# A recurrence and two feed-forward stages: from block 3 on every product in halves of 64 rows, two side by side

## The chip, the core and the metric

The kernel runs on one core of one Trainium2 chip. The metric is the device time of one execution in microseconds (us). TensorE does the matrix products, VectorE (DVE), ScalarE (ACT) and GpSimd (POOL) the elementwise work, SyncE (SP) mostly issues transfers. Weight loads of TensorE stand in the profile as an engine of their own, PEld.

## The reference: what is computed

A gated recurrence over 768 steps for 2 x 8 heads of width 40 gives an activation of 1536 tokens x 320. Two feed-forward stages follow, and they are what the change is about:

```python
# first stage: 4 experts, F = 1024, weighted by p
for e in range(E):
    h = np.maximum(x @ w1[e], 0.0)
    out += p[:, e:e + 1] * (h @ w2[e])
# second stage: d_ff = 1536
a = x @ w_a
b = x @ w_b
return (a * b @ w_out)
```

All in float32. The kernel takes each operand of a product as a high and a low part (`wh`, `wl` of the weights, `xh`, `xl` of the activation, `hh`, `hl` of the hidden values) and sums three of the four partial products.

## The kernel before, in words

**Blocks.** The hidden units are cut into 14 blocks. Blocks 0 to 7 belong to the first stage (two blocks of 4 x 128 hidden units for each expert), blocks 8 to 13 to the second (2 x 128 units each, with an `a` and a `b` product for each). Blocks 0 to 2 run interleaved with the recurrence, 256 tokens at a time (`Item`), and stay as they are. From block 3 on nothing else is left for TensorE; the tokens come in three groups `c` of 512. A **unit**, as the text calls it, is one block with one token group: 11 blocks x 3 groups = 33 units, 15 of the first stage and 18 of the second.

**First product of a unit (class `Pair`, method `a`).** Four sums, each in a PSUM bank of 128 x 512: four slices `f` of hidden units in the first stage, `b0, a0, b1, a1` in the second. The inner dimension is 320 = 128 + 128 + 64. A sum takes seven matmuls with all 128 rows (`mm_most`, line 214; the third row slice holds the 64 remaining weight rows twice, and `xh` there has the high part above the low part), and one more product, the low weights of the last 64 rows. For this last one two sums share a step: `mm_rest` (lines 219 and 220) issues a 64-row matmul in the upper half and another in the lower half of the array, for two different sums. `xq` is a copy of the 64 high rows on the lower partitions (`shift_x`). The sums 2 and 3 of a unit get theirs at its end, and together with them the sums 0 and 1 of the next unit get theirs as a first term (`begun`). Five units are named in `APART` and do without: there the last product is an eighth matmul of 128 rows (`mm_group`, line 207), and so it is where no `begun` sum was made.

**Eviction.** ReLU on ACT and the low part on DVE (lines 306, 307), or `bs`, `g`, `hh`, `hl` by turns on ACT and DVE in the second stage (lines 310 to 314).

**Second product (method `b`, lines 261 to 263).** For each of the four token tiles `t` of a unit three matmuls of 128 rows x 320 columns for each slice of hidden units: 48 in a unit of the first stage, 24 in one of the second. `Stream` runs it two items behind the first product. DVE then adds the sum to `acc` (lines 321, 783).

**Weights.** `piece1` and `piece2` are generators that load a piece of a block by a DMA on SP's queue (lines 86 and 104) and split it into `wh` and `wl` on ACT, DVE and POOL in the steps after. `Paced.step` advances them; `PACE` says after how many steps the next piece opens (1.5 for the first 32 pieces, which are blocks 4 to 7; 2.4 and 2.5 after). There are 8 steps in a unit of the first stage and 4 in one of the second. The raw pieces of the first stage go round two buffers, those of the second three. The order on each engine is the order in which the program writes its instructions.

**Between the stages** the 12 token tiles of `acc` are transposed back (`finish_x2`) and split. PSUM has eight banks: `Turns` takes four for the first product (`"a"`) and four for the second (`"b"`).

Of the kernel before, what the change touches and what calls it, by code (L numbers as in the profile page):

```python
# [18 lines left out]
P = 128  # L19
# [21 lines left out]
APART = ((NB1 - 1, 1), (NB1 - 1, 2), (NB1, 0), (NB1, 1), (NB1 + NB2 - 1, 2))  # L41
# [6 lines left out]
def mlstm_moe_kernel(ctx, tc, gates, qk, qc, kvo, dp, w1b, w2b, ident_d, bdmask_d, rsel_d, exp_d, out):  # L48
# [24 lines left out]
    def piece1(i, s, pool, lo_eng, apart=False):  # L73


        if s == 0:
            wblk[i] = (pool.tile([P, WB1], F32R, tag="wh", name=f"wh{i}"), pool.tile([P, WB1], F32R, tag="wl", name=f"wl{i}"))
        wh, wl = wblk[i]
        st = WB1 // NP1
        cs = slice(s * st, (s + 1) * st)  # L80
        if i < 3:
            at = (s if i == 0 else 8 + s if s < 2 else s) * st
            raw = sums[:, at:at + st]
        else:
            raw = rawp.tile([P, st], F32, tag="raw", name=f"raw{i}_{s}")
        nc.sync.dma_start(raw, w1b[i][:, cs])
        yield
        if apart:
            yield
        nc.scalar.copy(wh[:, cs], raw)  # L90
        yield
        lo_eng.tensor_tensor(wl[:, cs], raw, wh[:, cs].bitcast(F32), op=ALU.subtract)  # L92

    def piece2(i, s, pool):
# [9 lines left out]
        nc.sync.dma_start(raw.rearrange("p n w -> p (n w)"), w2b[i - NB1].bitcast(I32)[:, 2 * s * st:2 * (s + 1) * st])  # L104
# [21 lines left out]
    def split_x(ps, c, o):  # L126

        split_hi(ps, c, o)
        split_lo(ps, c, o)
# [9 lines left out]
    def shift_x(c):  # L139

        nc.gpsimd.dma_start(xq[c][64:128, :], xh[c][0:64, 2, :])
# [67 lines left out]
    def mm_most(ps, wh, wl, o0, c, start):  # L209

        k = lambda w, t: w[:, o0 + t * P:o0 + (t + 1) * P]
        prs = [(wh, 0, xh, 0), (wh, 1, xh, 1), (wh, 2, xh, 2), (wl, 0, xh, 0), (wl, 1, xh, 1), (wh, 0, xl, 0), (wh, 1, xl, 1)]
        for i, (w, t, x, u) in enumerate(prs):
            nc.tensor.matmul(ps, k(w, t), x[c][:, u, :], start=start and i == 0, stop=not start and i == len(prs) - 1)  # L214

    def mm_rest(psa, psb, wl, oa, ob, c, start):

        oa, ob = oa + 2 * P, ob + 2 * P
        nc.tensor.matmul(psa, wl[0:64, oa:oa + P], xh[c][0:64, 2, :], start=start, stop=not start)  # L219
        nc.tensor.matmul(psb, wl[64:128, ob:ob + P], xq[c][64:128, :], start=start, stop=not start)  # L220

    class Item:
# [5 lines left out]
        def a(self):  # L228
            blk, f, c, o, n = self.blk, self.f, self.c, self.o, self.n
            pa, ph = self.pools["a"], self.pools["h"]  # L230
            wh, wl = wblk[blk]
            self.hh = ph.tile([P, n], F32R, tag="hh", name="hh")
            self.hl = ph.tile([P, n], F32R, tag="hl", name="hl")
            if blk < NB1:
                ps = pa.tile([P, 512], F32, tag="a", name="psa")[:, :n]
                mm_group(ps, wh, wl, f * WF1, c, o, n)
                nc.scalar.activation(self.hh, ps, AF.Relu)  # L237
                nc.vector.scalar_tensor_tensor(self.hl, ps, 0.0, self.hh.bitcast(F32), op0=ALU.max, op1=ALU.subtract)  # L238
            else:
                pb = pa.tile([P, 512], F32, tag="a", name="psb")[:, :n]  # L240
                mm_group(pb, wh, wl, f * WF2 + 384, c, o, n)
                bs = ph.tile([P, n], F32, tag="bs", name="bs", bufs=2)
                nc.scalar.copy(bs, pb)
                ps = pa.tile([P, 512], F32, tag="a", name="psa")[:, :n]
                mm_group(ps, wh, wl, f * WF2, c, o, n)
                g = ph.tile([P, n], F32, tag="g", name="g", bufs=2)
                nc.vector.tensor_tensor(g, ps, bs, op=ALU.mult)
                nc.scalar.copy(self.hh, g)
                nc.vector.tensor_tensor(self.hl, g, self.hh.bitcast(F32), op=ALU.subtract)

        def b(self):
            blk, f, fi, nf, n = self.blk, self.f, self.fi, self.nf, self.n
            wh, wl = wblk[blk]
            off = f * WF1 + 384 if blk < NB1 else f * WF2 + 768
            if fi == 0:
                last = (blk, self.c) == (NB1 + NB2 - 1, 2)
                self.pools["bt"] = [self.pools[q].tile([P, DM], F32, tag=q, name="psy") for q in ("aabb" if last else "bbbb")[:n // P]]
# [8 lines left out]

    begun = {}

    class Pair(Item):

        def a(self):
            blk, f, c, one = self.blk, self.f, self.c, self.blk < NB1
            wh, wl = wblk[blk]
            pa, ph = self.pools["a"], self.pools["h"]
            new = lambda b, g: pa.tile([P, 512], F32, tag="a", name="psa" if b < NB1 or g % 2 else "psb")
            at = lambda b, g: g * WF1 if b < NB1 else g // 2 * WF2 + (g % 2 == 0) * 384
            self.q, ready = {}, [self]  # L280
            for g in [f] if one else [2 * f, 2 * f + 1]:
                if (blk, c, g) in begun:
                    self.q[g] = begun.pop((blk, c, g))
                    mm_most(self.q[g], wh, wl, at(blk, g), c, False)
                    continue
                self.q[g] = new(blk, g)
                if g < 2 or (blk, c) in APART:
                    mm_group(self.q[g], wh, wl, at(blk, g), c, 0, 512)
                    continue
                mm_most(self.q[g], wh, wl, at(blk, g), c, True)  # L290
                if g == 2:
                    ready = []
                    continue
                ready = [self.prev, self] if one else [self]
                p2 = self.prev.q[2] if one else self.q[2]
                mm_rest(p2, self.q[3], wl, at(blk, 2), at(blk, 3), c, False)
                nb, nc_ = (blk, c + 1) if c < 2 else (blk + 1, 0)
                for h in range(2):
                    begun[nb, nc_, h] = new(nb, h)
                mm_rest(begun[nb, nc_, 0], begun[nb, nc_, 1], wblk[nb][1], at(nb, 0), at(nb, 1), nc_, True)  # L300
            for it in ready:
                it.hh = ph.tile([P, 512], F32R, tag="hh", name="hh")
                it.hl = ph.tile([P, 512], F32R, tag="hl", name="hl")
                if one:
                    ps = it.q[it.f]
                    nc.scalar.activation(it.hh, ps, AF.Relu)  # L306
                    nc.vector.scalar_tensor_tensor(it.hl, ps, 0.0, it.hh.bitcast(F32), op0=ALU.max, op1=ALU.subtract)  # L307
                else:
                    bs = ph.tile([P, 512], F32, tag="bs", name="bs", bufs=2)
                    nc.scalar.copy(bs, it.q[2 * f])  # L310
                    g = ph.tile([P, 512], F32, tag="g", name="g", bufs=2)
                    nc.vector.tensor_tensor(g, it.q[2 * f + 1], bs, op=ALU.mult)  # L312
                    nc.scalar.copy(it.hh, g)
                    nc.vector.tensor_tensor(it.hl, g, it.hh.bitcast(F32), op=ALU.subtract)
# [447 lines left out]
    pools = {"a": Turns(ps_a2, ps_a), "b": Turns(ps_b2, ps_b), "h": hp2}  # L762
    todo, twice = [], {}

    def finish_x2(n):
        pt = pools["a"].tile([P, 512], F32, tag="a", name="pt_x2")
        pv = pt[:, 0:384].rearrange("p (k t) -> p k t", t=P)
        transpose_x(acc[n], twice[n], pv)
        split_x(pv, n // 4, (n % 4) * P)
        if n % 4 == 3:  # L770
            shift_x(n // 4)

    def done2(blk, n, ps):
        if blk < NB1:
            add_expert(blk, n, ps)
            if blk == NB1 - 1:
                twice[n] = hp2.tile([P, P], F32, tag="twice", name="twice", bufs=4)
                nc.scalar.copy(twice[n].rearrange("p (a b) -> p a b", a=2), acc[n][:, 256:].unsqueeze(1).to_broadcast([P, 2, 64]))
                todo.append(n)
# [13 lines left out]
    prev = None  # L793
    for blk in range(3, NB1 + NB2):
        nf = 4 if blk < NB1 else 2
        for c in range(3):
            for f in range(nf):
                ready = list(todo)

                def finish(k):  # L800
                    for n in ready[:k]:
                        ready.remove(n)
                        todo.remove(n)
                        finish_x2(n)

                def between():
                    paced.step()
                    if blk == NB1:
                        finish(2)

                item = Pair(blk, f, f, nf, c, 0, 512, pools, done2)
                item.prev, prev = prev, item
                stream.push(item, between)
                paced.step()
                finish(2)
    stream.flush()
# [102 lines left out]
```

## Time and profile before

| | us |
|---|---|
| median of 3 runs | 635.52 (635.46 to 637.06) |
| span of the profiled execution (its own time isn't listed beside the three) | 633.8 |
| TensorE busy | 621.0 (98%) |
| VectorE busy | 419.4 (66%) |
| ScalarE busy | 266.7 (42%) |
| GpSimd busy | 186.0 (29%) |

The profile is of one execution. Busy time of TensorE counts a matmul from its start to its modelled end, and matmuls overlap; how fast it really goes is read from the distance between the starts of two matmuls. The chain that ended last names, at each moment, the work that the end of the span hung on.

### The profile page before, as it was taken

How to read it: one execution, taken by the hardware profiler on the slowest of the kernel's cores; microseconds unless marked ns; L12 is line 12 of the kernel's file. 1: busy time of each engine (PE TensorE's matmuls, PEld its weight loads, DVE VectorE, ACT ScalarE, POOL GpSimd, SP SyncE). 2: the span in 40 equal slices, each digit the busy share in tenths (PEclk: the TensorE clock that was granted, in tenths of full speed). 3: DMA queues.
4: the chain of work that ended last, by engine and by line, in shares of the span. 5: the costliest groups of instructions: out<-in, count | busy, mean ns of one | idle time of the engine just before them, and what ended most of it. 6: DMA issues, size and time to landing. Idle time of an engine off the chain costs nothing.

```text
span 633.8 us, 10305 instructions
## 1 busy us (share of the span) xinstructions
PE 621.0 (98%) x3799; PEld 553.1 (87%) x3799; DVE 419.4 (66%) x860; ACT 266.7 (42%) x592; POOL 186.0 (29%) x223
## 2 busy tenths in 40 slices
PE   9898999999999999999999999999999999999997
PEld 6788999999999888888888888888888888888886
DVE  8889959596753244332788887888656776854344
ACT  6665464646333233332433344544543433422121
POOL 4686342424111011233233333333222222220000
PEclk9998999999999999999999999999999999999999
DMA  7882443435203122323221222221111111000003
GB/s 218 240 231 74 116 118 95 120 99 125 55 12 78 35 69 58 79 59 109 57 71 54 71 57 68 70 64 44 45 54 35 55 36 35 19 1 1 1 3 123
DMA packets 27967, 46.77 MB, mean 74 GB/s; under 512 B 3285, under 2 KB 17869, under 8 KB 27917
## 3 DMA queue, kind: packets, MB, share of 16 engines
q1 hardware_dynamic: 27437, 45.33, 26.2%
q0 software_dynamic: 480, 0.79, 0.6%
q8 instruction: 30, 0.49, 0.3%
q14 instruction: 20, 0.16, 0.1%
HBM read 43.35 MB, written 1.97 MB: 72 GB/s over the span
## 4 chain that ended last, share of the span: by engine, by line
PE 90%; DVE 6%; ACT 2%; issue 1%; POOL 1%; ACTq 0%; DVEq 0%; POOLq 0%
PE psa L214 20%; PE psa L207 14%; PE psy L261 13%; PE psy L263 11%; PE psy L262 11%; PE psb L214 8%; PE pt_y L503 3%; PE pt_c L485 2%; PE psb L207 2%; PE psb L219 1%; PE psa L219 1%; PE pt_i L509 1%; PE pt_a L475 1%; PE pt_w L590 1%; PE pt_u L553 1%
## 5 line engine op out<-in xcount | busy, mean ns | idle before, releaser
L261 PE MATMUL psy<-wh,hh 128*128 128x320 f32 x528 | 169.1, 320 | 0.6 <-DVE acc L321 0.6
L263 PE MATMUL psy<-wh,hl 128*128 128x320 f32 x528 | 163.2, 309 | 0.0
L262 PE MATMUL psy<-wl,hh 128*128 128x320 f32 x528 | 163.1, 309 | 0.0
L261 PEld LDWEIGHTS psy<-wh,hh 128*128 128x128 f32 x528 | 99.6, 189 | 15.5 <-issue 12.1
L262 PEld LDWEIGHTS psy<-wl,hh 128*128 128x128 f32 x528 | 99.7, 189 | 2.6
L263 PEld LDWEIGHTS psy<-wh,hl 128*128 128x128 f32 x528 | 99.4, 188 | 0.0
L307 DVE SCALAR_TENSOR_TENSOR hl<-psa,hh 128x512 fp32r<-128x512 f32 x60 | 40.2, 689 | 74.4 <-ACT hh L306 73.9
L124 POOL TENSOR_TENSOR wl<-tp,lf 128x272 fp32r<-128x272 f32 x48 | 38.8, 808 | 122.2 <-DVE tp L123 122.2
L214 PE MATMUL psa<-xh,wh 128*128 128x512 f32 x246 | 70.1, 393 | 0.0
L207 PE MATMUL psa<-xh,wh 128*128 128x256 f32 (+1 forms) x258 | 65.8, 309 | 0.4 <-ACT xh L132 0.4
L306 ACT ACTIVATE hh<-psa 128x512 fp32r<-128x512 f32 x60 | 34.5, 597 | 72.4 <-PE psa L214 41.3
L207 PE MATMUL psa<-xh,wl 128*128 128x256 f32 (+1 forms) x258 | 63.9, 302 | 0.0
L237 ACT ACTIVATE hh<-psa 128x256 fp32r<-128x256 f32 x72 | 27.6, 383 | 75.0 <-PE psa L207 73.5
L312 DVE TENSOR_TENSOR g<-psa,bs 128x512 f32<-128x512 f32 x36 | 24.8, 688 | 49.3 <-ACT bs L310 35.0
L121 POOL TENSOR_TENSOR lf<-lf,sq 128x272 f32<-128x272 f32 x48 | 37.2, 776 | 67.8 <-ACT wh L120 34.0
L92 POOL TENSOR_TENSOR wl<-raw,wh 128x352 fp32r<-128x352 f32 x28 | 26.6, 956 | 96.4 <-ACT wh L90 83.9
L214 PE MATMUL psa<-xh,wl 128*128 128x512 f32 x164 | 51.2, 393 | 0.0
L214 PE MATMUL psa<-xl,wh 128*128 128x512 f32 x164 | 50.8, 391 | 0.0
L238 DVE SCALAR_TENSOR_TENSOR hl<-psa,hh 128x256 fp32r<-128x256 f32 x72 | 30.3, 420 | 30.7 <-ACT hh L237 30.4
L214 PEld LDWEIGHTS psa<-xh,wh 128*128 128x128 f32 x246 | 44.0, 188 | 6.0
L310 ACT COPY bs<-psb 128x512 f32<-128x512 f32 x36 | 21.1, 587 | 62.7 <-PE psa L220 35.0
L207 PEld LDWEIGHTS psa<-xh,wh 128*128 128x128 f32 x258 | 45.2, 191 | 2.1 <-ACT xh L132 0.7
(139 smaller groups left out, 1168.0 us busy)
## 6 DMA issues: line engine op xcount, KB each, us to landing
raw<-in_w2b SPq DMA_DIRECT2D x48, 272.0 KB, 2.8
qk_t<-in_qk SPq DMA_DIRECT2D x16, 480.0 KB, 6.9
raw<-in_w1b SPq DMA_DIRECT2D x40, 176.0 KB, 2.3
acc<-in_w1b SPq DMA_DIRECT2D x24, 176.0 KB, 3.5
kvo_t<-in_kvo SPq DMA_DIRECT2D x10, 364.5 KB, 4.8
og_t<-in_kvo SPq DMA_DIRECT2D x6, 320.0 KB, 5.7
out<-acc SPq DMA_DIRECT2D x12, 160.0 KB, 1.8
qc_t<-in_qc SPq DMA_DIRECT2D x10, 180.0 KB, 3.6
```

The lines of the kernel that those rows point to most:

```text
L92: lo_eng.tensor_tensor(wl[:, cs], raw, wh[:, cs].bitcast(F32), op=ALU.subtract)
L121: nc.gpsimd.tensor_tensor(lf, lf, sq, op=ALU.mult)
L124: nc.gpsimd.tensor_tensor(wl[:, cs], tf, lf, op=ALU.add)
L207: nc.tensor.matmul(ps, l, r, start=(i == 0), stop=(i == len(prs) - 1))
L214: nc.tensor.matmul(ps, k(w, t), x[c][:, u, :], start=start and i == 0, stop=not start and i == len(prs) - 1)
L237: nc.scalar.activation(self.hh, ps, AF.Relu)
L238: nc.vector.scalar_tensor_tensor(self.hl, ps, 0.0, self.hh.bitcast(F32), op0=ALU.max, op1=ALU.subtract)
L261: nc.tensor.matmul(ps, lh, wh[:, off:off + DM], start=(fi == 0), stop=False)
L262: nc.tensor.matmul(ps, lh, wl[:, off:off + DM], start=False, stop=False)
L263: nc.tensor.matmul(ps, ll, wh[:, off:off + DM], start=False, stop=(fi == nf - 1))
L306: nc.scalar.activation(it.hh, ps, AF.Relu)
L307: nc.vector.scalar_tensor_tensor(it.hl, ps, 0.0, it.hh.bitcast(F32), op0=ALU.max, op1=ALU.subtract)
```

## The change

From block 3 on `Pair`, `mm_most`, `mm_rest`, `begun` and `APART` go. A unit's first product is `quad_a`: all its matmuls have 64 rows, and two always stand side by side, one on the upper 64 partitions (`UP`) and one on the lower (`DN`), for two different sums in two banks. In four phases the pairs of sums are (0,1), (2,3), (1,0), (3,2) as upper and lower; a phase has 8, 8, 7 and 7 pairs. The second product is `quad_b`, in the same way over token tiles. Since two halves may not be in one bank at once, the third and fourth phase must come behind the first and second: `leave` puts an empty instruction on SP that waits for the last matmul of a phase, and `behind` makes the first matmul of the phase two later wait for it. The second product of a unit runs behind the first product of the next unit; the evictions of slices 0 and 1 stand ahead of it, those of 2 and 3 in its middle. `hh` and `hl` have six buffers each. The DMAs of weight pieces from block 4 on are issued on ACT's queue. The transposes between the stages are done for four tiles at once, in banks of the second product. The last unit's second product is done with 128 rows.

```diff
-    def piece1(i, s, pool, lo_eng, apart=False):
+    def piece1(i, s, pool, lo_eng, apart=False, dma=None):
...
-        nc.sync.dma_start(raw, w1b[i][:, cs])
+        (dma or nc.sync).dma_start(raw, w1b[i][:, cs])
...
-        nc.sync.dma_start(raw.rearrange("p n w -> p (n w)"), w2b[i - NB1].bitcast(I32)[:, 2 * s * st:2 * (s + 1) * st])
+        nc.scalar.dma_start(raw.rearrange("p n w -> p (n w)"), w2b[i - NB1].bitcast(I32)[:, 2 * s * st:2 * (s + 1) * st])
...
+    def behind(later, earlier):
+        tc.add_manual_dep(later.ins, earlier.ins.name, mybir.DependencyInfo(mybir.DependencyClass.Sync, mybir.DependencyReason.DATA), reason="row groups take turns in a bank")
+
+    def leave(m):
+        word = nc.sync.nop()
+        behind(word, m)
+        return word
+
+    def quad_a(blk, c, ps, hook):
+
+        wh, wl = wblk[blk]
+        at = [g * WF1 if blk < NB1 else g // 2 * WF2 + (g % 2 == 0) * 384 for g in range(4)]
+        terms = [(wh, 0, xh), (wh, 1, xh), (wl, 0, xh), (wl, 1, xh), (wh, 0, xl), (wh, 1, xl), (wh, 2, xh), (wl, 2, None)]
+
+        def half(g, i, rows, start, stop):
+            w, t, x = terms[i]
+            x = x[c][rows, t, :] if x else xh[c][rows, 2, :] if rows.start == 0 else xq[c][rows, :]
+            o = at[g] + t * P
+            return nc.tensor.matmul(ps[g], w[rows, o:o + P], x, start=start, stop=stop)
+
+        left = {}
+        for k, (up, dn) in enumerate(((0, 1), (2, 3), (1, 0), (3, 2))):
+            n = 8 if k < 2 else 7
+            for i in range(n):
+                top = half(up, i, UP, k < 2 and i == 0, k >= 2 and i == n - 1)
+                low = half(dn, i, DN, k < 2 and i == 0, k >= 2 and i == n - 1)
+                if i == 0 and k >= 2:
+                    behind(top, left[k - 2])
+                if i == n - 1 and k < 2:
+                    left[k] = leave(low)
+                hook(8 * k + i)
+
+    def quad_b(blk, fs, nf, h, ps, hook):
+
+        wh, wl = wblk[blk]
+        pairs = ((0, 1), (2, 3), (1, 0), (3, 2)) if fs[0] % 4 == 0 else ((1, 0), (3, 2), (0, 1), (2, 3))
+        left = {}
+        for k, two in enumerate(pairs):
+            for f in fs:
+                off = f * WF1 + 384 if blk < NB1 else f * WF2 + 768
+                hh, hl = h[f]
+                for i, (l, w) in enumerate(((hh, wh), (hh, wl), (hl, wh))):
+                    start, stop = k < 2 and f == 0 and i == 0, k >= 2 and f == nf - 1 and i == 2
+                    ms = [nc.tensor.matmul(ps[t], l[rows, t * P:(t + 1) * P], w[rows, off:off + DM], start=start, stop=stop) for t, rows in zip(two, (UP, DN))]
+                    if k >= 2 and f == fs[0] and i == 0:
+                        behind(ms[0], left[k - 2])
+            if k < 2:
+                left[k] = leave(ms[1])
+            else:
+                hook()
 
...
-    pools = {"a": Turns(ps_a2, ps_a), "b": Turns(ps_b2, ps_b), "h": hp2}
...
+    pa, pb = Turns(ps_a2, ps_a), Turns(ps_b2, ps_b)
+    twice = {}
+
+    def finish_x2(c):
+        for n in range(4 * c, 4 * c + 4):
+            pt = pb.tile([P, 512], F32, tag="b", name="pt_x2")
+            pv = pt[:, 0:384].rearrange("p (k t) -> p k t", t=P)
+            transpose_x(acc[n], twice[n], pv)
+            split_x(pv, c, (n % 4) * P)
+        shift_x(c)
...
-    pieces = [piece1(i, s, slot[i], nc.vector if LOENG.get(i, ())[s:s + 1] == "v" else nc.gpsimd, True) for i in range(4, NB1) for s in range(NP1)]
+    pieces = [piece1(i, s, slot[i], nc.vector if LOENG.get(i, ())[s:s + 1] == "v" else nc.gpsimd, True, nc.scalar) for i in range(4, NB1) for s in range(NP1)]
...
+    def evict(blk, ps, f):
+        if blk >= NB1:
+            bs, g = (hp2.tile([P, 512], F32R, tag=t, name=n, bufs=HB).bitcast(F32) for t, n in (("hh", "bs"), ("hl", "g")))
+        hh, hl = (hp2.tile([P, 512], F32R, tag=t, name=t, bufs=HB) for t in ("hh", "hl"))
+        if blk < NB1:
+            nc.scalar.activation(hh, ps[f], AF.Relu)
+            nc.vector.scalar_tensor_tensor(hl, ps[f], 0.0, hh.bitcast(F32), op0=ALU.max, op1=ALU.subtract)
+        else:
+            nc.scalar.copy(bs, ps[2 * f])
+            nc.vector.tensor_tensor(g, ps[2 * f + 1], bs, op=ALU.mult)
+            nc.scalar.copy(hh, g)
+            nc.vector.tensor_tensor(hl, g, hh.bitcast(F32), op=ALU.subtract)
+        return hh, hl
...
+    units = [(blk, c) for blk in range(3, NB1 + NB2) for c in range(3)]
...
+    for u, (blk, c) in enumerate(units):
+        at = (14, 29) if blk >= NB1 else (7, 14, 22, 29)
+        ready = u - 2 - 3 * (NB1 - 4)
+
+        def hook(j):
+            if j in at:
+                paced.step()
+            if j == 15 and 0 <= ready < 3:
+                finish_x2(ready)
+
+        ps = [pa.tile([P, 512], F32, tag="a", name="psa" if blk < NB1 or g % 2 else "psb") for g in range(4)]
+        quad_a(blk, c, ps, hook)
+        h = [evict(blk, ps, f) for f in range(2)]
         nf = 4 if blk < NB1 else 2
...
+        if last:
+            b0, c0, h0 = last
+            n0 = len(h0)
+            py = [pb.tile([P, DM], F32, tag="b", name="psy") for _ in range(4)]
+            quad_b(b0, (0, 1), n0, h0, py, paced.step)
+        else:
+            stream.flush()
+        h += [evict(blk, ps, f) for f in range(2, nf)]
+        if last:
+            if n0 > 2:
+                quad_b(b0, (2, 3), n0, h0, py, paced.step)
+            for t in range(4):
+                done2(b0, 4 * c0 + t, py[t])
+        last = (blk, c, h)
+    blk, c, h = last
+    wh, wl = wblk[blk]
+    for t in range(4):
+        ps = pa.tile([P, 512], F32, tag="a", name="psy")[:, 0:DM]
+        for f in range(2):
+            hh, hl = (x[:, t * P:(t + 1) * P] for x in h[f])
+            off = f * WF2 + 768
+            nc.tensor.matmul(ps, hh, wh[:, off:off + DM], start=f == 0, stop=False)
+            nc.tensor.matmul(ps, hh, wl[:, off:off + DM], start=False, stop=False)
+            nc.tensor.matmul(ps, hl, wh[:, off:off + DM], start=False, stop=f == 1)
+        done2(blk, 4 * c + t, ps)
```

## Rows read from the trace of the kernel before

**Rows 1.** The page, engines: busy us, share of the span, instructions.

```profile
PE 621.0 (98%) x3799; PEld 553.1 (87%) x3799; DVE 419.4 (66%) x860; ACT 266.7 (42%) x592; POOL 186.0 (29%) x223
```

**Rows 2.** The page, chain that ended last: shares of the span by engine.

```profile
PE 90%; DVE 6%; ACT 2%; issue 1%; POOL 1%; ACTq 0%; DVEq 0%; POOLq 0%
```

**Rows 3.** Chain that ended last, 296 to 340 us: start us, us, what.

```profile
306.06 1.61 PE psa L214 x7
307.67 0.42 PE psa L219
308.10 0.23 PE psa L219
308.33 0.35 PE psy L261
...
318.26 0.47 DVE acc L321
...
318.87 0.38 PE psy L261
```

**Rows 4.** Timeline of PE, 300 to 309 us: start us, us, instruction, count.

```profile
300.78 0.30 PE L261 MATMUL psy<-wh,hh 128*128 128x320 f32 x1
...
302.53 0.39 PE L214 MATMUL psa<-xh,wh 128*128 128x512 f32 x1
...
305.90 0.86 PE L214 MATMUL psa<-xh,wh 128*128 128x512 f32 x3
...
307.60 0.49 PE L219 MATMUL psa<-xh,wl 64*128 64x512 f32 x1
...
307.94 0.39 PE L219 MATMUL psa<-xh,wl 64*128 64x512 f32 x1
...
308.52 0.30 PE L262 MATMUL psy<-wl,hh 128*128 128x320 f32 x1
```

**Rows 5.** Instructions of line 219: idle time of their engine before them, times.

```profile
  issue: 10.0, 28
```

**Rows 6.** Timeline of PEld (weight loads), 305.8 to 309.2 us.

```profile
307.60 0.18 PEld L219 LDWEIGHTS psa<-xh,wl 64*128 64x128 f32 x1 [0.35 <-issue]
307.60 0.18 PEld L220 LDWEIGHTS psa<-xq,wl 64*128 64x128 f32 x1
307.71 0.19 PEld L219 LDWEIGHTS psa<-xh,wl 64*128 64x128 f32 x1
307.71 0.19 PEld L220 LDWEIGHTS psa<-xq,wl 64*128 64x128 f32 x1
```

**Rows 7.** Timeline of PE, 104.3 to 107 us: short matmuls, each with its load.

```profile
104.42 1.91 PE L503 MATMUL pt_y<-kvo_t,w_t 128*128 128x82 f32 x16
106.17 0.87 PE L509 MATMUL pt_i<-cbd_t,qc_t 120*128 120x123 f32 x6
106.79 0.39 PE L261 MATMUL psy<-wh,hh 128*128 128x320 f32 x1
```

**Rows 8.** Windows: us, PE, PEld, DVE, ACT, POOL busy (x), PEclk, DMA share, GB/s.

```profile
100.00:120.00 20.00, 20.00 (x163) 19.91 (x163) 15.01 (x33) 10.12 (x21) 10.79 (x11) 1.00 0.50 126
...
340.00:360.00 20.00, 20.00 (x114) 17.71 (x113) 17.02 (x33) 8.73 (x21) 7.69 (x10) 1.00 0.26 70
360.00:380.00 20.00, 19.61 (x108) 16.67 (x107) 17.81 (x38) 7.02 (x18) 6.86 (x9) 1.00 0.22 57
```

**Rows 9.** Timeline of ACT, 307 to 309 us: idle before, and its releaser.

```profile
308.19 1.09 ACT L306 ACTIVATE hh<-psa 128x512 fp32r<-128x512 f32 x2 [1.88 <-PE psa L220]
```

**Rows 10.** Waits of SP's queue: waiter, releaser, us in total, times, longest.

```profile
SPq L104 <- DVE tp L115: 226.6, 45, 11.3
...
SPq L86 <- POOL wl L92: 61.7, 31, 9.3
```

**Rows 11.** Instructions of line 104: duration ns min/median/max, first and last start.

```profile
L104 SPq DMA_DIRECT2D raw<-in_w2b x48: 327/328/432, 296.7 to 542.3; - x48
```

**Rows 12.** The page, DMA issues: count, KB each, median us to landing.

```profile
raw<-in_w2b SPq DMA_DIRECT2D x48, 272.0 KB, 2.8
```

More of the change, by code (lines that the diff above doesn't have):

```diff
@@ L40 @@
 PACE = ((0, 1.5), (32, 2.4), (62, 2.5))
-APART = ((NB1 - 1, 1), (NB1 - 1, 2), (NB1, 0), (NB1, 1), (NB1 + NB2 - 1, 2))
+UP, DN = slice(0, 64), slice(64, 128)
+HB = 6
 NEG = -1.0e30
@@ L207, in mm_group @@
             nc.tensor.matmul(ps, l, r, start=(i == 0), stop=(i == len(prs) - 1))
[L209 to L220, printed above, removed]
+    def behind(later, earlier):
+        tc.add_manual_dep(later.ins, earlier.ins.name, mybir.DependencyInfo(mybir.DependencyClass.Sync, mybir.DependencyReason.DATA), reason="row groups take turns in a bank")
@@ L233, in a @@
             self.hl = ph.tile([P, n], F32R, tag="hl", name="hl")
[L234 to L249, printed above, removed]
+            ps = pa.tile([P, 512], F32, tag="a", name="psa")[:, :n]
+            mm_group(ps, wh, wl, f * WF1, c, o, n)
+            nc.scalar.activation(self.hh, ps, AF.Relu)
+            nc.vector.scalar_tensor_tensor(self.hl, ps, 0.0, self.hh.bitcast(F32), op0=ALU.max, op1=ALU.subtract)
         def b(self):
@@ L253, in b @@
             wh, wl = wblk[blk]
-            off = f * WF1 + 384 if blk < NB1 else f * WF2 + 768
+            off = f * WF1 + 384
             if fi == 0:
-                last = (blk, self.c) == (NB1 + NB2 - 1, 2)
-                self.pools["bt"] = [self.pools[q].tile([P, DM], F32, tag=q, name="psy") for q in ("aabb" if last else "bbbb")[:n // P]]
+                self.pools["bt"] = [self.pools["b"].tile([P, DM], F32, tag="b", name="psy") for _ in range(n // P)]
             for t in range(n // P):
@@ L265, in b @@
                     self.done(self.blk, self.c * 4 + self.o // P + t, ps)
[L267 to L314, printed above, removed]
@@ L761, in mlstm_moe_kernel @@
     ps_b2 = ctx.enter_context(tc.tile_pool(name="ps_b2", bufs=2, space=PS, reuse_waits="tile"))
-    pools = {"a": Turns(ps_a2, ps_a), "b": Turns(ps_b2, ps_b), "h": hp2}
[L763 to L771, printed above, removed]
+    pa, pb = Turns(ps_a2, ps_a), Turns(ps_b2, ps_b)
[7 more added lines that the diff above has]
+        shift_x(c)
     def done2(blk, n, ps):
@@ L778, in done2 @@
                 nc.scalar.copy(twice[n].rearrange("p (a b) -> p a b", a=2), acc[n][:, 256:].unsqueeze(1).to_broadcast([P, 2, 64]))
-                todo.append(n)
         elif blk == NB1:
@@ L794, in mlstm_moe_kernel @@
-    for blk in range(3, NB1 + NB2):
-        nf = 4 if blk < NB1 else 2
[L796 to L815, printed above, removed]
@@ L816, in mlstm_moe_kernel @@
-    stream.flush()
+    def evict(blk, ps, f):
[11 more added lines that the diff above has]
+        return hh, hl
@@ new lines, in mlstm_moe_kernel @@
+    units = [(blk, c) for blk in range(3, NB1 + NB2) for c in range(3)]
+    last = None
+    for u, (blk, c) in enumerate(units):
[9 more added lines that the diff above has]
+        h = [evict(blk, ps, f) for f in range(2)]
+        nf = 4 if blk < NB1 else 2
+        if last:
[12 more added lines that the diff above has]
+        last = (blk, c, h)
```

1 line of the change is left out of this document (removed).

## The prediction

> **What bounds the kernel now.** I read the page first. TensorE is busy for 98% of the span [rows 1] and carries 90% of the chain that ended last [rows 2]. So the question is how much of TensorE's time from block 3 on is something other than matmuls following each other. The share of busy time can't say that, since matmuls overlap in the records; the distance between starts can. In the timeline twelve matmuls of 320 columns go from 300.78 to 302.53, 0.146 us each [rows 4]. The chain has seven of 512 columns in 1.61, 0.230 each [rows 3]. I call these the short and the long step.
>
> What is lost stands between them, where a unit changes from 128 to 64 rows and back. In the chain seven long steps end at 307.67; then come 0.42 for the first pair of 64-row matmuls, 0.23 for the second pair, and 0.35 for the first matmul of 128 rows after them [rows 3]. At the steady steps that would be 0.23 + 0.23 + 0.146 = 0.61, and it is 1.00: 0.39 us go to the two changes, about 0.195 each. The weight load after such a change starts late, "issue" being all that is named, 28 times with 10.0 us for the way in alone [rows 5], 0.36 each time; that is longer than the delay because the last matmuls still run. The code gives 28 such units too: 33 less the five in APART. The second pair follows the first at 0.23, just the long step. In the two windows from 340 us on TensorE stands for 0 and 0.39 us in 20 [rows 8]. So the stage is bound by TensorE's steps.
>
> **The change, part by part.**
>
> *Steps of the first product.* Before, 944 matmuls of 128 rows and 56 pairs make 1000 long steps (33 units of 32 products, less two for each of the 56 pairs). After, 30 pairs in each of 33 units make 990. Ten long steps go: 10 x 0.23 = -2.3 us.
>
> *Changes of height.* In 28 units both changes go: 28 x 0.39 = -10.9. New ones: the first unit of block 3 is followed by the last two old items with 128 rows, three units hold transposes of 128 rows, the last unit ends with 128 rows, and there is the entry itself: 1 + 2 + 6 + 1 = 10 changes at 0.195, +2.0.
>
> *The second product.* 15 x 48 + 17 x 24 = 1128 short steps become pairs, 24 stay whole. The trace has no pair of 320 columns, so its length is bounded from both sides. From below: 192 more columns cost 0.084 us, 0.44 ns each, which leaves a fixed part of about 0.006 us in a step; if two halves hide that, all 2118 paired steps save 12.7 us. From above: a load takes about 0.109 us where loads follow each other (16 matmuls of 82 columns in 1.75 us, from 104.42 to 106.17) [rows 7]; two one after the other make 0.218 for a short step, +0.072 x 1128 = +81 us. I take the old steps, no gain and no loss: the row that is nearest is the pair itself. There the loads of both halves start together at 307.60 and the next two together at 307.71 [rows 6], so a pair of loads took 0.11, as one does, and 0.11 fits under 0.146.
>
> *Turns over SP.* 160 turns (2 x 33 in first products, 4 x 15 + 2 x 17 in second). Path: the phase's last matmul ends, SP passes its empty instruction, TensorE goes on. A handover from TensorE to ACT took 0.09 us (the second half of the pair ends at 308.10, ACT starts at 308.19) [rows 4, 9]; two make 0.2. The cover is the phase between: 8 x 0.23 = 1.84 us in a first product, 6 x 0.146 = 0.88 in a second, less the 0.16 by which a short matmul's record outlasts its step. So 0.5 us to spare, cost nothing. Behind a waiting instruction on SP stand later turns and, for the last three units alone, the output transfers; a transfer ahead of a turn waits for DVE's addition, at most some 1 us for two units. The handover to SP and back isn't shown; at 0.5 us each way it would cost (1.0 + 0.16 - 0.88) x 94 turns = 26 us, below nothing it can't come, since it only adds.
>
> *DMAs on ACT's queue.* 32 pieces of the first stage and 48 of the second, 0.33 us of issue each on SP [rows 11], 26 us on an engine that is busy 7 to 9 us in 20 there [rows 8]. On SP these issues stood for long: 226.6 us for DVE reading an earlier piece, 61.7 us in 31 times for POOL's subtraction [rows 10]. SP had nothing else to do; on ACT the evictions queue behind, and for those the next unit's banks. What hides it: a unit's four banks are written again only after a second product of 24 or 48 short steps, 3.5 or 7.0 us. In the second stage an issue stands some five steps behind the reads that free its buffer, so it should find it free. In blocks 4 to 7 the issue stands in the same step as the subtraction it waits for. Five pieces in a unit at 2.0 us (61.7 / 31) would be 10 us of 14 and with the rest of ACT's work 1 to 2 us too much in each of the six units over which these pieces go: between 0 and +10 us. I take 0: ACT stood before as well, for the data that the same ring of two buffers brings late, and what it waits in the issue it waits less in the copy.
>
> *DVE in blocks 5 to 7* is busy 17.0 to 17.8 us in 20 [rows 8]; the same work in units some 3% shorter is 88 to 92%. A piece now is asked for later, landing 2.8 us after [rows 12], and DVE may stand for it: 0 to 1 us in each of nine units. I take 0. Additions that now and then came late (at 318.26 the chain goes over DVE's `acc` and the next matmul takes 0.38 for 0.15) [rows 3] have a whole first product of 6.9 us as cover after the change; I don't count that gain.
>
> *Sum.* -2.3 - 10.9 + 2.0 = -11.2. The profiled execution has a span of 633.8; the median of the runs, 635.5, is 1.7 above it, which is what lies around the span. 633.8 - 11.2 = 622.6 of span, **624.3** us.
>
> **Rivals.**
>
> 1. *The loads of the two halves go in turn* (slower). Place: the second product, where a step of 0.146 us has to hold two loads; a long step holds 0.218. For: the trace shows pairs of loads only by twos, after a stop, and none with 320 columns. Against: those pairs start together [rows 6]. Price: 0.218 for 0.146, +81 us, 705 us. It decides from 0.156: 11.2 / 1128 = 0.010 in a short step eats the gain. Chance 0.10. The Trainium skill, "TensorE: Matmul & The Clock Gate", Part 2, gives TensorE one read port for weights and a load time that goes by columns, not rows, which would be this case; the trace disagrees for the pairs of before (both loads start at 307.60, the next two at 307.71 [rows 6]).
> 2. *TensorE can't take four instructions in a short step* (slower), 0.037 each. For: the densest rows are 44 loads and matmuls in 2.37 us, 0.054 each [rows 7], and 326 in 20 us, 0.061 each [rows 8]. Against: loads and columns explain both. Price: at 0.054 a short step takes 0.216, +0.070 x 1128 = +79, 703 us; at 0.061 every step takes 0.244, 0.098 x 1128 + 0.014 x 990 = +124, 749 us. Chance 0.09. The same part of that page says that without hardware decode the sequencer spends about 62 ns on each matmul; were it so for loads too, a step would be 0.248, an estimate from that page. The 0.054 of rows 7 speaks against it, though instructions that were waiting in a queue could hide it over so short a stretch.
> 3. *The fixed part is hidden* by the other half: 624.3 - 12.7 = 612. For: two halves, each with its own load. Against: the second pair at 0.23 [rows 3]. Chance 0.09.
> 4. *Evictions and pieces come late*: ACT held by its own issues in the first six units (up to +10), DVE short of time in the nine after (up to +9), a turn now and then. 627 to 643. For: the rows of SP's long waits and DVE at 89%. Against: the cover named above. Chance 0.20, of which 0.08 still faster, 0.06 the same, 0.06 slower.
>
> **The numbers.** Forecast 0.52, at 620 to 628 by itself. A measurement can tell 0.3%, 1.9 us, from no change. Faster: 0.52 + 0.09 + 0.08 = 0.69; same 0.06; slower 0.10 + 0.09 + 0.06 = 0.25. Rivals 1 and 2 lie above 700 and are the 0.19 that the range leaves out; it takes in rivals 3 and 4 with a little beyond for what they leave unpriced: 609 to 644.
>
> **What would show it.** Right: in the timeline pairs of 320 columns at 0.146 and of 512 at 0.23, both loads of a pair within 0.01; no weight load with 0.36 of "issue" ahead of it but around transposes; no waits of TensorE on SP; block 3 on shorter by 11 us. Wrong: short pairs at 0.156 or more; idle time of TensorE ended by SP, or by ACT and DVE at the first matmuls of a unit in blocks 3 to 7; ACT standing in its DMA issues for more than 3.5 us.

## The result and the profile after

| | before | after |
|---|---|---|
| median (lowest to highest), us | 636.29 (635.46 to 637.10) | 621.45 (621.31 to 623.11) |
| ratio, 95% interval | | 0.9768 (0.975 to 0.9785) |
| profiled execution, us | | 621.56 |
| its span, us | 633.8 | 619.9 |

The change makes the kernel faster by 14.8 us; 624.3 was forecast, in a range of 609 to 644. The span after lies 1.7 us under the time of its execution, as the forecast took it.

The page of the kernel after, engines and shares of the chain that ended last (they answer to [rows 1, 2]), and its issues of the moved DMAs, to [rows 12]:

```profile
PE 607.9 (98%) x5850; PEld 573.3 (92%) x5851; DVE 421.7 (68%) x860; ACT 265.5 (43%) x592; POOL 186.5 (30%) x223
...
PE 90%; DVE 4%; DMA 3%; ACT 1%; issue 1%; SPq 1%; POOL 0%; DVEq 0%; ACTq 0%; POOLq 0%
...
raw<-in_w2b ACTq DMA_DIRECT2D x48, 272.0 KB, 2.7
```

TensorE has 2051 more matmuls and 2052 more loads, is still busy for 98%, and DVE, ACT and POOL have the work they had. The share of busy time tells nothing here; the chain does. After, from 290 to 330 us (start us, us, what), answering to [rows 3]:

```profile
291.85 6.83 PE psa L228 x60
298.68 7.04 PE psy L253 x96
305.71 6.83 PE psa L228 x60
312.54 7.04 PE psy L253 x96
319.57 6.83 PE psa L228 x60
```

A first product is one piece of 60 matmuls, a second one of 96, and nothing stands between them: no 0.42 and 0.35 at a change of height, no DVE. Two halves make a pair, so a long pair takes 6.83 / 30 = 0.2277 us and a short one 7.04 / 48 = 0.1467. The timeline of PE, 300 to 312 us, has the pairs themselves, answering to [rows 4]:

```profile
305.06 0.36 PE L253 MATMUL psy<-wh,hh 64*128 64x320 f32 x2
...
305.50 0.68 PE L228 MATMUL psa<-xh,wh 64*128 64x512 f32 x4
...
307.11 0.39 PE L228 MATMUL psa<-xh,wl 64*128 64x512 f32 x1
307.17 0.39 PE L228 MATMUL psa<-xq,wl 64*128 64x512 f32 x1
```

The halves don't start together but 0.06 us apart. The queue that passes the turns waits for TensorE, 159 times in these two rows of its waits, answering to [rows 10]; among TensorE's waits there is none on SP.

```profile
SPq L214 <- PE psy L253: 213.3, 94, 5.8
SPq L214 <- PE psa L228: 185.7, 65, 11.8
```

The windows of two units, one of block 6 and one of block 7, columns as in [rows 8]:

```profile
361.15:375.01 13.86, 13.86 (x159) 13.86 (x157) 12.85 (x26) 6.65 (x16) 5.56 (x7) 1.00 0.25 64
375.01:389.04 14.03, 14.03 (x159) 14.03 (x157) 13.49 (x27) 5.40 (x13) 6.04 (x8) 1.00 0.28 78
```

TensorE never stands, with DVE busy for 93 and 96%. And one unit is 0.17 longer than the other, which nobody waits for; the experiments come back to it.

**Block 3 on gained more than the spans differ by.** Nothing is changed ahead of block 3, but the profile after comes there later. The chain around 26 us and at the start of block 3, first the kernel before:

```profile
26.56 0.95 PE psa L207 x8
...
29.52 0.96 PE psa L207 x8
...
210.94 1.86 PE psa L207 x8
```

and after:

```profile
26.54 1.61 PE psa L208 x8
...
31.08 0.98 PE psa L208 x8
...
212.75 7.19 PE psa L228 x60
```

The same eight matmuls at 26.5 us take 1.61 instead of 0.95, and what follows is late by 1.6 already at 31 us. The windows from 25 to 30 us, columns as in [rows 8], of before, of after, and of the kernel before with its weight loads on ACT's queue (one of the experiments; the same program up to there):

```profile
25.00:30.00 5.00, 5.00 (x42) 4.94 (x42) 3.88 (x7) 3.15 (x10) 5.00 (x5) 1.00 0.90 287
```

```profile
25.00:30.00 5.00, 5.00 (x31) 4.98 (x31) 3.32 (x6) 2.51 (x9) 5.00 (x5) 0.66 0.89 269
```

```profile
25.00:30.00 5.00, 5.00 (x31) 4.98 (x31) 3.62 (x7) 2.73 (x9) 5.00 (x5) 0.66 0.86 261
```

The granted clock is 1.00 in the first and 0.66 in the others, so part of that stretch ran at the lower of the clock's two levels, 1.2 instead of 2.4 GHz; in the 5 us ahead TensorE had been busy for 3.0 in all three. That goes with the execution and not with the change: the third kernel does its products as before and shows the same 0.66, at 636.91 us, and the four runs of before lie at 635.5 (two) and at 637.1 (two), a step of 1.6. From block 3 on the gain in the two profiles is (633.8 - 210.9) - (619.9 - 212.75) = 15.7 us, against 11.2 in the sum.

### The profile page after: what moved, and what is told of

It is laid out like the page before. It is cut to its first block, busy times and chain, and to the rows that moved or that the text cites. A ratio compares the mean times of both kernels' runs of the same rounds, so it can differ in the third digit from the quotient of the medians.

```text
span 619.9 us, 14426 instructions
## 1 busy us (share of the span) xinstructions
PE 607.9 (98%) x5850; PEld 573.3 (92%) x5851; DVE 421.7 (68%) x860; ACT 265.5 (43%) x592; POOL 186.5 (30%) x223
## 4 chain that ended last, share of the span: by engine, by line
PE 90%; DVE 4%; DMA 3%; ACT 1%; issue 1%; SPq 1%; POOL 0%; DVEq 0%; ACTq 0%; POOLq 0%
PE psy L253 27%; PE psa L228 26%; PE psb L228 11%; PE psa L208 10%; PE psy L287 3%; PE psy L289 3%; PE psy L288 3%; PE pt_y L480 2%; PE pt_c L462 1%; DMA qc_t<-in_qc 1%; DMA og_t<-in_kvo 1%; PE pt_i L486 1%; DMA kvo_t<-in_kvo 1%; DVE qs_t L349 1%; PE pt_a L452 1%; PE pt_u L530 1%
## 5 line engine op out<-in xcount | busy, mean ns | idle before, releaser
L228 PE MATMUL psa<-xh,wh 64*128 64x512 f32 x576 | 133.5, 390 | 0.0
L253 PE MATMUL psy<-wl,hh 64*128 64x320 f32 x752 | 127.2, 305 | 0.0
L253 PE MATMUL psy<-wh,hh 64*128 64x320 f32 x752 | 127.1, 305 | 0.0
L253 PE MATMUL psy<-wh,hl 64*128 64x320 f32 x752 | 127.0, 305 | 0.0
L228 PE MATMUL psa<-xh,wl 64*128 64x512 f32 x414 | 96.3, 389 | 0.0
L228 PE MATMUL psa<-xl,wh 64*128 64x512 f32 x384 | 84.6, 389 | 0.0
L228 PEld LDWEIGHTS psa<-xh,wh 64*128 64x128 f32 x576 | 79.1, 184 | 5.9 <-issue 0.9
L253 PEld LDWEIGHTS psy<-wh,hh 64*128 64x128 f32 x752 | 81.6, 184 | 0.8
L253 PEld LDWEIGHTS psy<-wl,hh 64*128 64x128 f32 x752 | 81.3, 184 | 0.8
L253 PEld LDWEIGHTS psy<-wh,hl 64*128 64x128 f32 x752 | 81.5, 184 | 0.0
```

The source lines that it names most:

```text
L228: return nc.tensor.matmul(ps[g], w[rows, o:o + P], x, start=start, stop=stop)
L253: ms = [nc.tensor.matmul(ps[t], l[rows, t * P:(t + 1) * P], w[rows, off:off + DM], start=start, stop=stop) for t, rows in zip(two, (UP, DN))]
```

## The experiments

**Does a change of height cost what the sum says?** Two kernels ask from both sides. The first is the kernel before with the first terms of the next unit put behind the second product, so that a unit changes height four times instead of twice:

```diff
                 nb, nc_ = (blk, c + 1) if c < 2 else (blk + 1, 0)
-                for h in range(2):
-                    begun[nb, nc_, h] = new(nb, h)
-                mm_rest(begun[nb, nc_, 0], begun[nb, nc_, 1], wblk[nb][1], at(nb, 0), at(nb, 1), nc_, True)
+
+                def later():
+                    for h in range(2):
+                        begun[nb, nc_, h] = new(nb, h)
+                    mm_rest(begun[nb, nc_, 0], begun[nb, nc_, 1], wblk[nb][1], at(nb, 0), at(nb, 1), nc_, True)
+                self.later = later
...
                 stream.push(item, between)
+                if hasattr(item, "later"):
+                    item.later()
```

> The kernel before, with its second pair of 64-row matmuls (the first terms of the next unit's sums 0 and 1) moved behind the 128-row matmuls of the second product: four changes of height in a unit instead of two, the same matmuls. Theory (each change costs 0.195 us): 28 x 0.39 = +10.9 us, 647 us. Rival (the cost belongs to the pairs themselves or to their data, not to the change): no difference, 636 us.

Measured: 648.27 (646.56 to 649.78), 1.0183 of the kernel before (1.0158 to 1.0207), which had 637.06 here: +11.2 us, or 0.20 for each of the 56 changes added. In its chain each pair that stands alone takes 0.43 for 0.23, and the step after it 0.34 for 0.15:

```profile
297.11 0.43 PE psa L219
297.54 0.34 PE psy L261
...
299.49 0.43 PE psa L219
299.93 1.81 PE psa L214 x7
```

The second is the changed kernel with its second product in whole height, for which `quad_b` becomes the old loop over `t` and `f`:

```diff
-        for k, two in enumerate(pairs):
+        for t in range(4):
             for f in fs:
...
-                    ms = [nc.tensor.matmul(ps[t], l[rows, ...], w[rows, ...], ...) for t, rows in zip(two, (UP, DN))]
+                    nc.tensor.matmul(ps[t], l[:, ...], w[:, ...], ...)
```

> The changed kernel with its second product in 128 rows again, so that each unit has two changes of height, and no turns in the second product. Theory: 32 stretches of 128 rows are entered and left, less the changes that are there anyway: 62 x 0.195 = +12 us over 621.5, 633 to 634 us, with steps of 0.146 as before. Rival (pairs of 320 columns are faster or slower than whole matmuls and bring part of the result): the short steps differ between the two traces, and the time lies 5 us or more from 633.5.

Measured: 633.75 (632.17 to 633.81), 0.9946 of the kernel before (0.9926 to 0.9965): 12.3 us of the gain are gone. Its chain has whole-height steps as long as the pairs and 0.20 more at each end of a product (7.24 for 7.04, 7.03 for 6.83):

```profile
300.42 7.24 PE psy L250 x48
307.66 7.03 PE psa L228 x56
```

So halves of 320 columns aren't faster than whole steps: 48 of either take 7.04, less the 0.20 of a change. The gain is that the height hardly ever changes.

**What do the turns cost without cover?** The changed kernel, each pair of sums in a second product followed at once by the same pair with the halves exchanged:

```diff
-        pairs = ((0, 1), (2, 3), (1, 0), (3, 2)) ...
+        pairs = ((0, 1), (1, 0), (2, 3), (3, 2)) ...
...
-                        behind(ms[0], left[k - 2])
+                        behind(ms[0], left[k - 1])
```

> The changed kernel with the phases of the second product in the order (0,1), (1,0), (2,3), (3,2): each of its 94 turns over SP now follows the phase it waits for at once and has no cover. Theory (a turn's path is the matmul's tail 0.16, two handovers of 0.05 to 0.1, and the load that can't be taken ahead, 0.11): 0.35 to 0.45 each, 33 to 42 us more, 655 to 664 us. Rival (SP answers slowly, 0.5 us each way, and the cover was nearly used up): 1.2 us each, 735 us. Second rival (the wait costs nothing even so): 622 us.

Measured: one run, 657.25, 35.8 over the changed kernel. Part of that lies ahead of block 3, which begins later here than in the profile after:

```profile
214.42 2.76 PE psa L228 x21
```

From block 3 on the two profiles differ by (655.5 - 214.4) - (619.9 - 212.75) = 34.0, 0.36 for each of 94 turns. The chain goes through SP at every turn, and the load behind it (timeline of PEld) names SP:

```profile
293.22 2.04 PE psy L253 x24
295.26 0.02 issue
295.28 0.02 SPq L214
295.30 0.04 issue
295.34 2.04 PE psy L253 x24
```

```profile
295.34 0.19 PEld L253 LDWEIGHTS psy<-wh,hh 64*128 64x128 f32 x2 [0.36 <-SPq L214]
```

12 short pairs take 1.76 in steady steps; here they come every 2.12, so 0.36 is lost. The row shows the path: 0.08 lies between the last matmul's end and the load, SP's own 0.02 among it. The rest would be the last matmul's own running out and the first load, which steady steps hide; no run takes these two apart.

**Does the queue of the weight loads matter?** Both ways: the changed kernel with its loads back on SP, and the kernel before with its loads on ACT.

```diff
-        nc.scalar.dma_start(raw.rearrange(...), ...)
+        nc.sync.dma_start(raw.rearrange(...), ...)
...
-    ... else nc.gpsimd, True, nc.scalar) ...
+    ... else nc.gpsimd, True, nc.sync) ...
```

> The changed kernel with the weight loads back on SP's queue, ahead of the turns that follow them in the program. Theory (the turns have 0.5 to 1.8 us of cover, and a load finds its buffer free or nearly so): 622 to 630 us, TensorE standing only in the blocks where two raw buffers go round (4 to 7). Rival (loads that wait on SP hold up the turns everywhere, so that the move to ACT is what makes the change possible): 640 us or more.

> The kernel before with one part of the change alone: the weight pieces from block 4 on are issued on ACT's queue. Theory (ACT has room, and the evictions wait for nothing long): within 1.5 us of the kernel before. Rival (ACT's issues wait for POOL and DVE and hold the evictions, with the shorter cover that the kernel before has): 3 us or more slower, TensorE standing before line 261 or 214 in blocks 3 to 7.

Measured: 621.35 in one run, as after; and 636.94 (635.38 to 638.59), 0.9999 of the kernel before (0.9982 to 1.0016). Neither way counts. In the second one ACT's waits for the data of its pieces are nearly those of before (17.6 us in 13 times there, in the same row):

```profile
ACT wh L90 <- DMA raw<-in_w1b: 16.5, 12, 3.2
```

Beside it stand 5.4 us in three times for DVE's subtraction, which before has none of, so the waiting isn't only moved. In the profile after that row is

```profile
ACT wh L91 <- DVE wl L93: 7.5, 3, 4.1
```

The longest, 4.1, is over the 3.5 us that the prediction named as a sign of wrong; at 234 us a load that ACT had to issue stood until DVE had done with its buffer. TensorE didn't wait for it. So the forecast's 0 for this part holds and its upper end of +10 doesn't; that the loads must leave SP for the turns' sake is refuted as well.

**Do the loads of two halves go in turn?** At 320 columns that couldn't be told, if a pair of loads were no longer than the step. So the short pairs of the changed kernel were cut into two of 160 columns each, with a load for each. Against what was expected, this kernel's sums don't come out right, and the runs don't show why; number and size of the matmuls, and so the pace that is asked for here, are as said.

```diff
-  ms = [nc.tensor.matmul(ps[t], l[...], w[rows, off:off + DM], ...) for t, rows in zip(two, (UP, DN))]
+  ms = [nc.tensor.matmul(ps[t][:, q:q + 160], l[...], w[rows, off + q:off + q + 160], ...) for q in (0, 160) for t, rows in zip(two, (UP, DN))]
```

> The changed kernel with each paired matmul of the second product cut into two of 160 columns, each with its own load: 2256 pairs in place of 1128, the same result. It measures how fast pairs can follow each other. Theory (the loads of the two halves go side by side, 0.109 for both): a pair at 0.11 to 0.12, 2256 x 0.115 - 1128 x 0.1467 = +94 us, 700 to 730 us. Rival 1 (loads in turn, hidden so far by nothing shorter than 0.1467): 0.218 at the most, up to 950 us; anything between shows how far they overlap. Rival 2 (neither loads nor instructions bind, columns alone): 0.08, 636 us.

Measured: one run, 707.71. Its chain:

```profile
292.50 6.85 PE psa L228 x60
299.35 10.68 PE psy L253 x192
```

96 pairs in 10.68 us are 0.111 each, two loads and two matmuls. That is one load's own time where loads follow each other, 0.109 by [rows 7]: the two loads go side by side, and four instructions pass in 0.111, 0.028 each. Rivals 1 and 2 are refuted with room to spare. It also shows what carries a short step: halving its columns takes only 0.035 off, and what is left is a load's 0.109.

**Is DVE's slack real, and how much is it?** The changed kernel, `hl` formed twice in blocks 5 to 7:

```diff
+            for _ in range(2 if blk >= 5 else 1):
-            nc.vector.scalar_tensor_tensor(hl, ps[f], 0.0, ...)
+                nc.vector.scalar_tensor_tensor(hl, ps[f], 0.0, ...)
```

> The changed kernel, in which DVE forms hl twice in blocks 5 to 7: 36 more operations of 0.68 us, 2.7 us in each of the nine units. In the changed kernel DVE is busy 11.7 to 13.5 us in these units of 13.86 to 14.05 us. Theory (DVE costs nothing there because 0.5 to 2 us of each unit are left, and no more than that): the units are stretched to DVE's own time, 15.3 us in the mean, TensorE waits on DVE again, and some 8 to 15 us are lost: 629 to 636 us. Rival (evictions lie off the path, since the second product runs a unit behind, and the pieces' splits give way): under 1 us lost, 621 to 622.5 us.

Measured: one run, 636.03, 14.6 us slower. From 305 to 405 us DVE is busy for 96% and TensorE now stands for 4.5 us (in the changed kernel DVE is busy for 88.93 us and TensorE for all 100.00):

```profile
305.00:405.00 100.00, 95.49 (x1013) 87.11 (x1011) 96.14 (x183) 35.26 (x87) 33.27 (x41) 0.98 0.22 59
```

```profile
PE psa L228 <- DVE hl L777: 6.0, 8, 0.8
```

The granted clock in this window is 0.98 and 1.00 in the changed kernel: 3.4 us from 383.6 on ran at the lower level, after TensorE had stood time and again, and up to 1.7 of the loss may be that. The 36 operations are 24.5 us of work, so some 10 to 12 were still free. Being a unit behind gives DVE no more than that: over nine units its own time nearly sets the pace.

**What makes one unit 0.17 longer than the next?** In the profile after, a first product takes 6.82 to 6.86 in blocks 4 to 6 and 9 to 11, 7.00 in blocks 3, 7 and 12, and 6.88 to 6.89 in 13 and in the one unit of 8 without transposes; block 13 begins a first product at 581.50 and the second at 588.39:

```profile
581.50 0.23 PE psb L228
...
588.39 3.51 PE psy L253 x48
```

That goes by the pool in which a block's weights lie, `wp0`, `wp1` and `wx`. Pool `wp1` lies at the far end of SBUF, at a start address that leaves 96 on division by 128 bytes; `wp0` and all activations leave 32, and `wx` 96. A tile of 64 bytes at the front moves everything but `wp1`:

```diff
+    const.tile([P, 16], F32, name="pad")
     ident = const.tile([P, P], F32, name="ident")
```

> The changed kernel with 64 bytes per partition left free at the front of SBUF, so that everything but the weights of blocks 3, 7 and 12 lies 64 bytes further. In the changed kernel the first product of a unit takes 6.83 us in blocks 4 to 6 and 9 to 11, 7.00 in 3, 7 and 12, and 6.89 in 13. Theory A (the place of the weights relative to the activation, modulo 128 bytes, sets it): blocks 3, 7 and 12 fall to 6.83. Theory R (it is the far end of SBUF, above 192 KB in a partition, that is slower to load weights from): nothing changes, 7.00 stays and the time is 621.5.

The other kernel opens `wx` ahead of `hp2` and `cvt`, so that its blocks get another address:

```diff
+    wx = ctx.enter_context(tc.tile_pool(name="wx", ...))
     hp2 = ctx.enter_context(tc.tile_pool(name="hp2", ...))
     cvt = ctx.enter_context(tc.tile_pool(name="cvt", ...))
-    wx = ctx.enter_context(tc.tile_pool(name="wx", ...))
```

> The changed kernel with the pool of blocks 8 and 13 opened ahead of the pools of the hidden values and the conversions, so that these weights lie at 146 KB to 164 KB instead of 189 KB to 207 KB in a partition. Theory R (weights above 192 KB load slower): block 13's first product falls from 6.89 to 6.83 us a unit, block 8 likewise, 6 x 0.06 = 0.4 us in all, 621 us. Theory A (alignment): the weights now lie at the same place modulo 128 bytes as those of blocks 4 to 6, so the same; with the run before the two are told apart. Rival (it is something in the block's own work): 6.89 stays.

Measured: 619.84 and 621.1, one run each. With the tile, blocks 3, 7 and 12 take 6.83 and blocks 8 and 13 stay; with `wx` first block 13 and the last unit of block 8 shorten by 0.04 to 0.06 and blocks 3, 7 and 12 stay. Then both together, a pad of 32 bytes, and the pad in the kernel before:

> The changed kernel with both shifts of the two looks before: a 64-byte tile at the front of SBUF and the pool wx opened ahead of hp2 and cvt, so that the weight blocks of all three pools and the activations have the same remainder (96) on division of their addresses by 128 bytes. Theory A (a long pair takes 0.2333 us where weights and activations differ by 64 in that remainder, 0.2277 where they agree): every first product of a whole unit takes 6.83 us in blocks 3, 7 and 12 (7.00 in the changed kernel), and blocks 8 and 13 lose their 0.02 to 0.06 us more per unit too; 621.45 - 9 x 0.17 - 6 x 0.04 = 619.7 us (619.2 to 620.2), a ratio to the kernel before of about 0.974. Rival (the pad's look was scatter between executions): 621.0 to 622.0 us.

> The changed kernel with a tile of 32 bytes instead of 64 at the front of SBUF: the activations and the blocks in wp0 then lie at a remainder of 64 on division by 128 bytes, wp1 stays at 96, wx comes to 0. Theory A1 (any difference in the remainder costs): blocks 3, 7 and 12 stay at 7.00 us for a first product, 621.0 to 621.9 us in all. Theory A2 (only a difference of 64 costs): 6.83 us there and 6.83 to 6.89 in blocks 8 and 13 that now differ by 64; 619.5 to 620.3 us. Theory A3 (it is the activations' own remainder, not the difference): blocks 4 to 6 change as well, by up to 0.17 us per unit.

> The kernel before with the 64-byte tile at the front of SBUF. Theory A (the remainder of the addresses sets part of the long step, whatever the height of the matmul): the steps of 128 rows in blocks 3, 7 and 12 fall from 0.233 us to 0.231 or less, so about 9 units x 28 to 30 x 0.0024 to 0.005 = 0.6 to 1.4 us are gained, a ratio to the kernel before of 0.998 to 0.999. Rival (it concerns only pairs of 64-row matmuls): no change, a ratio of 1.000, and 0.233 us stays in these blocks.

Measured with both: 619.62 (619.52 to 619.78), 0.972 of the kernel before (0.9706 to 0.9735), the fastest kernel here. The chain of its block 7, and the same units after:

```profile
374.35 6.83 PE psa L229 x60
381.17 7.04 PE psy L254 x96
388.20 6.83 PE psa L229 x60
```

```profile
375.01 7.00 PE psa L228 x60
382.01 7.03 PE psy L253 x96
389.04 7.00 PE psa L228 x60
```

With 32 bytes: one run, 621.37, and blocks 3, 7 and 12 stay at 7.00, here the first of block 7:

```profile
374.86 6.99 PE psa L229 x60
```

So it isn't a difference of 64 alone that costs (A2), and as blocks 4 to 6 stay at 6.82 to 6.86, not the activations' own place either (A3). What holds of A1: in all these kernels weights and activations with the same remainder are fast. The remainders don't say what a difference costs: the weights in `wx` differ by 64 too, in the profile after and with either pad, and their blocks take 6.88 or 6.89, not 7.00. The second product doesn't care (7.03 to 7.04 in all of them).

The kernel before with the pad: 634.56 (634.46 to 637.63), 0.996 (0.9948 to 0.9972). That is more than the 0.6 to 1.4 us expected, but it compares runs at different granted clocks (0.996 in most of these, 0.993 to 0.995 in most of those of before here). From block 3 on, where both profiles are at 1.00, it is 1.1 us: (633.8 - 210.9) - (635.9 - 214.1), with the start of block 3 in the chain of the run with the pad

```profile
214.10 1.84 PE psa L208 x8
```

In its chain seven steps of 128 rows in block 3 take 1.61, and 1.63 in the kernel before:

```profile
219.53 1.61 PE psa L215 x7
```

```profile
219.81 1.63 PE psa L214 x7
```

In block 3 and the first units of block 7 the mean distance between starts is 0.233 to 0.234 before and 0.230 to 0.231 with the pad, in block 12 0.233 to 0.234 and 0.229: the place of the weights counts for whole steps as well.

## Why the prediction was right

**Steps.** Ten long steps fewer, 2.3 us: right in number. *Mis-sized:* the steps themselves. By the distances between the starts of all matmuls a long step was 0.2307 in the mean before and a long pair is 0.2296, so 990 of them give another 1.1 us, of which the sum had none. In blocks 4 to 6 the two are 0.2308 and 0.2276; why a pair of 512 columns is the shorter isn't shown.

**Changes of height.** Right, and the bulk of it. By the same distances the 28 units lost 11.1 us, 0.40 each, not 10.9; the kernel with four changes says 11.2 for as many again, the one with whole second products 12.3 for 32 units. The ten new ones cost 1.9, against 2.0. The prediction's three pieces were read from the chain, which goes by ends. By starts the loss is spread otherwise: from the last long step at 307.28 on the distances are 0.32, 0.34, 0.33 and 0.26, so the second pair follows the first at 0.34 [rows 4] and not at 0.23. The total is the same, but the 0.23 was no evidence against rival 3. "Issue" as what holds a load at line 228 is down to five times, 0.9 us in all, where [rows 5] had 28 times and 10.0 for one of the two changes:

```profile
  issue: 0.9, 5
```

The Trainium skill says under "TensorEngine Tiling (Array Packing)", Key Properties, that changing the tiling mode drains TensorE. The runs agree, at 0.20 us a change; the page gives no figure.

**The second product.** "The old steps, no gain and no loss" was right, 0.1467 against 0.146. Rival 1, for which the prediction had read the Trainium skill's one read port for weights ("TensorE: Matmul & The Clock Gate", Part 2) as loads in turn, is refuted by the pairs of 160 columns; the argument of [rows 6], pairs that start together, was the right one. Rival 2 fell with the same run (0.028 us an instruction). Rival 3 didn't come: at 320 columns 64 rows beside 64 take as long as 128, and at 512 columns the mean step lost 0.001, not 0.006.

**Turns.** Cost 0, right. The uncovered turn had been put together as two handovers, 0.2, and the 0.16 by which a short matmul's record outlasts its step; 0.36 was measured, so the cover of 0.88 leaves the 0.5 us that was named. The bound of +26 us was too careful.

**DMAs on ACT's queue.** 0, right, shown by both exchanges; the sign that was named against it, a stand of over 3.5 us, came and cost nothing. **DVE in blocks 5 to 7.** 0, right, but with less room than "88 to 92%" says: 93 and 96% in the units above. Rival 4 didn't come, and the run with `hl` twice shows what it would have been.

**The term that was left out** is the largest miss. The sum named a late addition [rows 3] and didn't count its end. TensorE's waits before had

```profile
PE psy L261 <- DVE acc L321: 0.6, 3, 0.2
PE psb L207 <- DVE xh L137: 0.6, 1, 0.6
```

and after neither. A wait of 0.2 is not its price. At each of the three the next matmul started 0.31 to 0.39 late and the one behind it another 0.08, 1.3 us in all; at the fourth it was 0.8. These four make 2.1 us. At four more places, in the units named in `APART` and around them, another 0.9 was lost that is gone after. With 1.1 for the long steps, 0.2 and 0.1 for the old and new changes, and 0.2 behind the last matmul that is 4.6, for the 4.5 us by which block 3 on gained more than forecast. The clock early in the execution took 1.7 back in this profile, so that the time came out 2.8 under the forecast, not 4.5: that the forecast lies so near is in part luck.

## What to carry to other kernels

Look for what an engine loses between two kinds of step, not only in them: 11 us lay at 56 places at which TensorE changed its height, and they went by giving nearly every product one height, although the products themselves hardly became faster. Where turns must be passed between engines, put a phase of other work between giving and taking; 0.36 us is the price of one without it here, and nothing with it. And price a stall by the distance of the next starts, not by the wait that the profile names.

## What the runs showed of the hardware that was not expected

**Halves out of step.** Two halves of a pair start 3 to 4 ns apart in the first unit, 0.057 us apart from 222 to 408 us, and 3 ns from the first transposes on; with both shifts of the address experiments it is 0.110 in that middle stretch. A pair takes the same time either way (a unit of blocks 9 to 11, with 30 pairs of 512 columns and 24 of 320, comes every 10.34 us, which is 6.82 + 3.52). The prediction wanted both loads of a pair within 0.01 as a sign; that sign failed and meant nothing.

**The address of the weights.** Pairs of 512 columns take 0.2277 us (0.2289 at the most in the mean of a unit without transposes) where the weights' and the activations' addresses leave the same remainder on division by 128 bytes. Where the remainders differ they take 0.2333 in blocks 3, 7 and 12 (by 64 or by 32) and 0.2296 in block 13 (by 64), so the remainders alone don't set it. 64 bytes of padding and an exchanged order of pools gave 1.8 us. Why is open: the runs tell the places apart, not what reads them.
